# Last chunk of a long convolution: the place of one eviction on ScalarE, and a sum handed from VectorE to an accumulating transfer

## The chip, the cores and the metric

The kernel runs on one core of a Trainium2 chip. The metric is the device time of one execution in microseconds (us), given as the median of several runs. A core has five engines with an instruction queue each: TensorE (PE in the profile, its weight loads PEld), VectorE (DVE), ScalarE (ACT), GpSimd (POOL) and SyncE (SP). Matrix products land in PSUM and are copied out ("evicted") by ScalarE or VectorE. Transfers are issued by SP (queue q1 in the profile) or POOL (queue q0) and are carried out by sixteen DMA engines that all queues share.

## The reference

For 2048 positions and 1024 channels, two branches are mixed by a gate g = sigmoid(x · gate_w) of each position.

- Branch a is a diagonal state-space layer: `Bu = x @ B_bar.T`, the recurrence `h[t] = Lam_bar * h[t-1] + Bu[t]` (complex, 1024 states), then `a = 2 * Re(h @ C.T) + x * Dskip`.
- Branch b is a convolution over the whole sequence: k is convolved with four taps for each channel and multiplied by v, the product kv is convolved with `ssm_k` along the positions by a Fourier transform of twice the length, `kv * ssm_D` is added, and the result is multiplied by x.
- The output is `g * a + (1 - g) * b`, 1 x 2048 x 1024 in bf16.

## The kernel before

**Branch b** goes over the channels in eight chunks of 128. For a chunk, matmuls against tables of sines and cosines give the spectra K of the filter and V of kv, in four blocks. `products` (line 676) forms the spectrum G of their product on VectorE. It is a generator: each `yield` is a place where the caller may put other work. It multiplies first component by V into G, then the first component of the shifted blocks into W1 (one half of the work tile `wkh`), and adds W1 to blocks 1 to 3 of G. In all other chunks that sum is an accumulating transfer (`gather`, line 126, issued by POOL: 128 partitions x 2 x 1536 elements, 768 KB). In the last chunk, with `by_dma=False`, it is a tensor_tensor of 128x3072 on VectorE, four multiplications later. Blocks 2 and 3 of G then get one more sum, and four more operations of 128x2048 end the chunk's G. `inverse` (line 728) turns G back: eight matmuls into a PSUM tile `psz`, an eviction `cv` on ScalarE, a store of `cv` to a DRAM scratch by SP, and the same once more for the odd tiles.

**Branch a** is done in units of a block of 512 positions and a group of 256 states. `Bu(i)` makes two PSUM tiles named `both` (16 matmuls each, weights from `BT[g]`, which hold B for group g: first the eight matmuls with the real part, then eight with the imaginary part). ScalarE evicts each in two halves into `U`. `turn_U` (line 884) then scales U into `Q` on ScalarE in two steps, each followed by a `gather` of Q into U; the second transfer waits until the first has landed. VectorE runs the scans, and `Cy` multiplies by C: PSUM tile `psy`. `turn_C(pi)` (line 1266) mixes real and imaginary part of C's tile pi: two ScalarE operations into `m`, two more in place, and two gathers. C's first three tiles are called `CTa` in the trace.

**Order.** `put` (line 92) keeps each engine's instructions in the order of the program. PSUM is a pool of four tiles used in turn (line 81), so a PSUM tile is free again when the tile four places earlier has been evicted. The change lies in the block after the loop over the first seven chunks, which interleaves the last chunk's products (`prod`), the inverse of chunk 6 (`back`), the scaling of C's first two tiles (`turning[0]`, `turning[1]`), the gates of two position blocks (`gate`, 64 small matmuls in two PSUM tiles `p`, four tiny ScalarE operations) and the units Bu(6), Bu(7) and Bu(8). Before it, SP has been given the transposing loads of `CTa` 0 and 1, `BT[2]`, `BT[3]`, `CTa` 2 and `CT3`, in the order: CTa 0, BT[2], CTa 1, BT[3] (real, imaginary), CTa 2, CT3; then the two stores of `cv`, then the x of the last position block (`load_xT(3)`). Bu(7) is the first unit that uses BT[3].

Of the kernel before, what the change touches and what calls it, by code (L numbers as in the profile page):

```python
# [9 lines left out]
ALU = mybir.AluOpType  # L10
# [10 lines left out]
def kernel(  # L21
# [64 lines left out]
    def ps2(shape, name):  # L86
        return psum.tile(shape, F32, name=name, tag="ps")
# [4 lines left out]
    def put(eng, f, *a, **kw):  # L92
        with tc.issue_after(prev[eng]) if eng in prev else nullcontext():
            i = f(*a, **kw)  # L94
        prev[eng] = getattr(i, "ins", i)

    def mm(o, l, r, first, last):
        put("pe", nc.tensor.matmul, o, lhsT=l, rhs=r, start=first, stop=last)

    def bc(ap, shape):  # L100
        return ap.to_broadcast(shape)
# [3 lines left out]
    def tt(o, a, b, op):  # L105
        put("dve", V.tensor_tensor, out=o, in0=a, in1=b, op=op)
# [10 lines left out]
    def act(o, i, **kw):  # L117
        put("act", nc.scalar.activation, out=o, in_=i, **kw)
# [4 lines left out]
    def move(o, i):  # L123
        put("sp", nc.sync.dma_start, out=o, in_=i)

    def gather(o, i):
        put("pool", nc.gpsimd.dma_start, out=o, in_=i, accum_op=ALU.add)
# [122 lines left out]
    def load_xT(tb, halves=(0, 1), held=False):  # L250
        if tb not in xTs:
            xTs[tb] = (xt_pool if tb in (1, 2) else xt_first).tile([128, ND, TB], BF16, name="xT", tag="xT")
        for h in halves:
            if held:
                hold(xTs[tb][:, 0, h * HB:h * HB + 1])
            load_t(xTs[tb][:, :, h * HB:(h + 1) * HB], xf[tb * TB + h:(tb + 1) * TB:2, :])
# [201 lines left out]
    def turn_table(g):  # L458

        hr = u4([128, 2, 2, HB], F32, "hr")  # L460
        h, y = hr[:, 0], hr[:, 1]
        n = y.bitcast(I32)
        for o, rate in ((h, thn), (n, nthn)):
            for j in range(2):
                act(o[:, j], trow[0][:, 0:HB], func=ACT.Identity, scale=rate[:, 2 * g + j:2 * g + j + 1])
        yield
        gather(h, n)
        yield
        act(y, h, func=ACT.Abs)
        act(TS[:, 2 * g:2 * g + 2], h, func=ACT.Sin, scale=TWO_PI)  # L470
        act(TC[:, 2 * g:2 * g + 2], y, func=ACT.Sin, bias=pih, scale=-TWO_PI)
# [137 lines left out]
    def spectrum(which, c):  # L609
        if which == "K" and c % 2 == 0:  # L610

            t = BT[2].rearrange("p c d q -> p (c d q)")
        elif which == "G":
            t = whole[c] = g_pool.tile([128, 4096], BF16, name="G")
        else:
            t = kv_pool.tile([128, 4096], BF16, name=which + "h", tag="kvh")
        k = 2 if c == 0 else 1
        return [t[:, h * 4096 // k:(h + 1) * 4096 // k].rearrange("p (c b f d) -> p c b f d", c=2, b=4, d=128)
                for h in range(k)]
# [53 lines left out]
                    mm(ps[:, cc], tab[:, mt, fsl], eo[cc][:, mt], mt == 0, mt == 1)  # L673
            act(of_tile(VH[c], fi), ps, func=ACT.Copy, scale=2.0 / 1024.0)

    def products(c, h=0, home=u4, by_dma=True):

        if c not in GH:
            GH[c] = spectrum("G", c)
        K, Vt, G = (x[c][h].rearrange("p c b f d -> p c b (f d)") for x in (KH, VH, GH))  # L680
        w = K.shape[3]
        T2s = kv_pool.tile([128, 4096], BF16, name="t2", tag="kvh") if c == NC - 1 else BT[3].rearrange("p c d q -> p (c d q)")
        T2 = T2s[:, h * 2048:h * 2048 + 8 * w]
        W1, W2 = (WK[:, i, h * 1536:h * 1536 + 6 * w] for i in range(2))

        def mult(a, k, room, t=None):

            full = [128, 2, 4 - a, w]
            if t is None:
                t = room.rearrange("p (c b x) -> p c b x", c=2, x=w)  # L690
            tt(t, bc(K[:, k:k + 1, a:a + 1], full), Vt[:, :, 0:4 - a], ALU.mult)
            return t

        mult(0, 0, None, G)
        yield
        n1 = mult(1, 0, W1)
        if by_dma:
            gather(G[:, :, 1:], n1)
        yield
        t2 = mult(0, 1, T2)  # L700
        yield
        n2 = mult(1, 1, W2)
        if not by_dma:
            tt(G[:, :, 1:], G[:, :, 1:], n1, ALU.add)
        if c == NC - 1:
            yield
        n3 = mult(2, 1, home([128, 4 * w], BF16, "t"))
        tt(t2[:, :, 1:], t2[:, :, 1:], n2, ALU.add)
        n2 = mult(3, 1, home([128, 2 * w], BF16, "t"))
        tt(t2[:, :, 2:], t2[:, :, 2:], n3, ALU.add)  # L710
        n1 = mult(2, 0, W2[:, 0:4 * w])
        n3 = mult(3, 0, W2[:, 4 * w:])
        tt(t2[:, :, 3:], t2[:, :, 3:], n2, ALU.add)
        tt(n1[:, :, 1:], n1[:, :, 1:], n3, ALU.add)
        yield
        tt(G[:, :, 2:], G[:, :, 2:], n1, ALU.add)
        yield
        tt(t2[:, 1], G[:, 0], t2[:, 1], ALU.subtract)
        tt(t2[:, 0], G[:, 1], t2[:, 0], ALU.add)
        if c == 0 and h == 0:  # L720
            return
        lo, hi = ((t2[:, :, :, 0:256], t2[:, :, :, 256:512]) if c > 0 else
                  [T2s[:, i * 2048:(i + 1) * 2048].rearrange("p (c b x) -> p c b x", c=2, x=256) for i in range(2)])
        to = whole[c].rearrange("p (a c b x) -> p a c b x", a=2, c=2, b=4)
        tt(to[:, 0], lo, hi, ALU.subtract)
        tt(to[:, 1], lo, hi, ALU.add)

    def inverse(c):

        del GH[c]  # L730
        G = whole.pop(c).rearrange("p (a c b f d) -> p a c b f d", a=2, c=2, b=4, d=128)
        for par in range(2):
            ps = ps2([128, 2, 4, 128], "psz")
            for j in range(2):
                tl = 2 * par + j
                for fi in range(2):
                    for cc, tab in enumerate((CI, SI)):
                        mm(ps[:, j], tab[:, fi, tl * 128:(tl + 1) * 128], G[:, par, 1 - cc, :, fi],
                           fi == 0 and cc == 0, fi == 1 and cc == 1)
            cv = cv_pool.tile([128, 2, 4, 128], BF16, name="cv")  # L740
            act(cv, ps, func=ACT.Copy)
            move(cv_scr[c, :, 2 * par:2 * par + 2], cv)
            yield
# [16 lines left out]
    def gate(tb):  # L760
        psg = ps2([128, 2, 512], "p")[:, 0, 0:4]
        for tl in range(4):
            for dt_ in range(ND):
                mm(psg[:, tl:tl + 1], xTs[tb][:, dt_, tl * 128:(tl + 1) * 128], gwb[:, dt_:dt_ + 1],
                   dt_ == 0, dt_ == ND - 1)
        gates_of(slice(tb * 4, tb * 4 + 4), psg)
# [81 lines left out]
    turns_U = {}  # L848
# [208 lines left out]
    def step(gen):  # L1057
        next(gen, None)

    def run(gen):  # L1060
        for _ in gen:
            pass

    def steps(gen, n):
        for _ in range(n):
            step(gen)
# [35 lines left out]
    step(turns)  # L1102
    taps(1, dg1)
    p0 = products(0, 0)
    steps(p0, 3)
    tv = times_v(1)
# [17 lines left out]
    for c in range(NC - 1):  # L1124
        n, nn = c + 1, c + 2
        if c == 0:
# [3 lines left out]
            load_BT(0, 0)  # L1130
            load_xT(0, (0,))
            p1 = products(0, 1)
            fwd_K(n, (0, 1))
            step(p0)
# [25 lines left out]
        if c == 6:  # L1160
            put("pool", nc.gpsimd.tensor_copy, stamp, xTs[2][:, 0, 0:HB + 1:HB])
        tabs, back, prod = turn_table(c - 1) if c <= NG else none, inverse(c - 1), products(c)
        step(old)
        step(tabs)
# [91 lines left out]
    c = NC - 1  # L1256
# [36 lines left out]
    with tc.tile_pool(name="fin", bufs=1, side="right") as fin:  # L1293

        count = iter(range(16))

        def room(shape, dt, name):
            return fin.tile(shape, dt, name=name, tag=f"fin{next(count)}")

        prod, back = products(c, 0, room, False), inverse(c - 1)  # L1300
        run(old)
        steps(prod, 3)
        run(turns_U[3])
        run(next(tiles))
        steps(turning[0], 2)
        step(back)
        steps(turning[1], 2)
        run(back)
        gate(1)
        gate(2)  # L1310
        steps(prod, 2)
        b6, b7 = Bu(6)
        run(b6)
        run(b7)
        run(turns_U[6])
        run(turning[0])
        run(turning[1])
        run(prod)
        b8, b9 = Bu(7)
        run(b8)  # L1320
        run(b9)
        load_xT(3)
        b10, b11 = Bu(8)
        run(b10)
        run(b11)
    back = inverse(c)
# [208 lines left out]
```

## Time and profile before

| What | Value |
|---|---|
| time, median of 3 runs | 381.42 us (381.31 to 384.8) |
| the profiled execution's own time | 382.42 us |
| its span, first to last instruction | 380.6 us |
| PE busy | 370.4 us, 97% of the span |
| DVE busy | 369.1 us, 97% |
| ACT busy | 309.2 us, 81% |
| POOL busy | 81.8 us, 21% |
| granted TensorE clock | 0.999 |
| queue q1 (issued by SP) | 45.64 MB |
| queue q0 (issued by POOL) | 25.17 MB |

The span runs from the first to the last instruction of the core; the execution's time has 1.82 us around it. Busy shares are means over the span: two engines at 97% do not say which of them sets the end. A timeline row gives start, duration, engine, line (nearly all L94, the helper that records every operation), operation, `output<-inputs`, shapes and count, and in brackets the idle time before it with what ended it. Rows of one kind that follow each other are merged, so a merged row's duration covers all of them. Rows of the SP and POOL queues give the issue of a transfer, not its landing.

### The profile page before, as it was taken

To read this page: it belongs to the slowest core of one execution; us is meant where nothing else is said; L and a number is where in the kernel's file an instruction comes from. 1 tells how busy PE (TensorE), PEld (TensorE's weight loads), DVE (VectorE), ACT (ScalarE), POOL (GpSimd) and SP (SyncE) were. 2 spreads that over 40 slices of the span, in tenths; PEclk is the share of its full clock that TensorE was granted. 3 is DMA by queue.
4 is the path that set the end of the run, shared out by engine and by line. 5 is a ranking of instruction groups with operands and counts; after the bars stand their busy time and mean duration, and the time that the engine had idled before them with its cause. 6 is when DMAs were issued, how large, how long until landed. Compare 5 with 4: busy or idle time off the path is not lost.

```text
span 380.6 us, 6635 instructions
## 1 busy us (share of the span) xinstructions
PE 370.4 (97%) x2419; PEld 198.2 (52%) x2453; DVE 369.1 (97%) x593; ACT 309.2 (81%) x475; POOL 81.8 (21%) x111
## 2 busy tenths in 40 slices
PE   7999999999999999999989999999999999999996
PEld 4656357575574846644444444444444444444442
DVE  8899999999999999999999999999999999999995
ACT  5889996988979999786969699997988968948611
POOL 4011030110301103031002212223425322535000
PEclk9999999999999999999999999999999999999999
DMA  7979999999999998959998999976999999998902
GB/s 167 167 112 246 221 215 173 245 208 217 199 168 214 219 198 167 195 140 153 171 215 180 209 207 240 245 153 126 183 236 164 246 249 206 171 246 141 219 1 110
DMA packets 126403, 71.78 MB, mean 189 GB/s; under 512 B 104665, under 2 KB 107489, under 8 KB 126370
## 3 DMA queue, kind: packets, MB, share of 16 engines
q1 hardware_dynamic: 111232, 45.64, 56.2%
q0 software_dynamic: 12976, 25.17, 38.8%
q10 hardware_dynamic: 2162, 0.54, 0.8%
q8 instruction: 19, 0.31, 0.3%
q14 instruction: 14, 0.11, 0.1%
HBM read 15.48 MB, written 8.39 MB: 63 GB/s over the span
## 4 chain that ended last, share of the span: by engine, by line
PE 69%; DVE 15%; DMA 6%; issue 4%; ACT 3%; SPq 2%; ACTq 1%
PE psy L94 29%; PE both L94 17%; PE psk L94 6%; DVE BT L94 5%; DVE wkh L94 5%; PE psv L94 4%; PE taps L94 3%; PE foldk L94 3%; PE psz L94 3%; PE even L94 2%; DMA kT<-kT 2%; PE odd L94 2%; DVE G L94 2%; SPq L94 2%; ACT Vh L94 2%
## 5 line engine op out<-in xcount | busy, mean ns | idle before, releaser
L94 PEld LDWEIGHTS <-BT 128*128 128x128 bf16 x640 | 62.0, 98 | 49.5 <-issue 1.4
L94 PE MATMUL both<-xT,BT 128*128 128x512 bf16 x375 | 83.2, 379 | 1.4 <-ACT cv L94 1.0
L94 POOL DMA_DIRECT2D U<-Q x26 | 26.7, 1040 | 86.3 <-ACT Q L94 42.2
L94 PEld LDWEIGHTS <-hb 128*128 128x128 bf16 x256 | 25.0, 98 | 30.2 <-issue 0.5
L94 PEld LDWEIGHTS <-U 128*128 128x128 bf16 x240 | 23.5, 98 | 28.3
L94 PE MATMUL psy<-CT,hb 128*128 128x512 bf16 x157 | 36.5, 379 | 0.1
L94 ACT ACTIVATE Vh<-psv 128x1024 bf16<-128x1024 f32 x32 | 30.7, 1034 | 6.0 <-PE psv L94 6.0
L94 PE MATMUL psy<-CT,U 128*128 128x512 bf16 x148 | 34.6, 379 | 0.2
L94 DVE TENSOR_TENSOR_SCAN W<-rv,init,A 128x256 bf16<-128x256 f32 x48 | 32.1, 729 | 0.0
L94 POOL DMA_DIRECT2D G<-wkh x8 | 9.7, 1218 | 100.0 <-DVE wkh L94 100.0
L94 ACT ACTIVATE U<-both 128x512 bf16<-128x512 f32 x44 | 24.2, 594 | 8.3 <-PE both L94 8.0
L94 ACT ACTIVATE Q<-U,lam 128x512 bf16<-128x512 bf16 (+1 forms) x52 | 29.9, 612 | 0.0
L94 PE MATMUL psk<-eok,SF 128*128 128x384 bf16 (+1 forms) x119 | 28.2, 354 | 0.3
L94 PEld LDWEIGHTS <-SF 128*128 128x128 bf16 x184 | 18.0, 98 | 19.2 <-issue 0.5
L94 PE MATMUL psz<-G,CI 128*128 128x512 bf16 x64 | 24.3, 379 | 0.1
L94 PE MATMUL psz<-G,SI 128*128 128x512 bf16 x64 | 24.3, 379 | 0.0
L94 PE MATMUL psy<-CTa,hb 128*128 128x512 bf16 x94 | 22.6, 379 | 0.2
L94 PE MATMUL taps<-dg,kT 128*128 128x128 bf16 (+1 forms) x352 | 21.3, 207 | 1.4 <-DMA kT<-in_B_k_dram 1.0
L94 PEld LDWEIGHTS <-kT 128*128 128x128 bf16 x352 | 20.6, 98 | 3.2 <-DMA kT<-in_B_k_dram 2.0
L94 DVE TENSOR_TENSOR wkh<-BT,Vh 128x3072 bf16<-128x3072 bf16 (+4 forms) x20 | 21.8, 1109 | 0.0
L94 DVE TENSOR_TENSOR wkh<-Kh,Vh 128x3072 bf16<-128x3072 bf16 (+2 forms) x16 | 21.2, 1347 | 0.0
L94 PE MATMUL psy<-CTa,U 128*128 128x512 bf16 x87 | 20.6, 379 | 0.1
(230 smaller groups left out, 846.8 us busy)
## 6 DMA issues: line engine op xcount, KB each, us to landing
U<-Q POOLq DMA_DIRECT2D x26, 256.0 KB, 5.2
G<-wkh POOLq DMA_DIRECT2D x6, 768.0 KB, 8.8
cv_scr<-cv SPq DMA_DIRECT2D x16, 256.0 KB, 7.7
kn<-in_B_ssm_k_dram SPq DMA_DIRECT2D x5, 512.0 KB, 3.8
v<-in_B_v_dram SPq DMA_DIRECT2D x5, 512.0 KB, 6.4
out_dram<-m SPq DMA_DIRECT2D x8, 256.0 KB, 4.6
BT<-cv_scr SPq DMA_DIRECT2D x7, 256.0 KB, 6.3
out_dram<-BT SPq DMA_DIRECT2D x7, 256.0 KB, 2.0
```

Source lines behind the costliest of these rows:

```text
L94: i = f(*a, **kw)
```

## The change

In the last chunk the sum of W1 into blocks 1 to 3 of G becomes a `gather`, issued right after W1's multiplication, as in the other chunks; the tensor_tensor goes, and with it the parameter `by_dma`. `run(turns_U[3])` (eight ScalarE operations into Q, two gathers) comes ahead of the first three steps of `prod` in the program, so that on POOL its two gathers stand ahead of the new one; VectorE's and ScalarE's own orders are not touched by that. `run(back)`, which holds the second half of the inverse of chunk 6 (eight matmuls, the eviction `cv` on ScalarE, SP's store), comes ahead of `steps(turning[1], 2)`, the first two ScalarE operations on C's tile 1. PE's and SP's orders stay as they are.

```diff
-    def products(c, h=0, home=u4, by_dma=True):
+    def products(c, h=0, home=u4):
...
         n1 = mult(1, 0, W1)
-        if by_dma:
-            gather(G[:, :, 1:], n1)
+        gather(G[:, :, 1:], n1)
         yield
         t2 = mult(0, 1, T2)
         yield
         n2 = mult(1, 1, W2)
-        if not by_dma:
-            tt(G[:, :, 1:], G[:, :, 1:], n1, ALU.add)
         if c == NC - 1:
             yield
...
-        prod, back = products(c, 0, room, False), inverse(c - 1)
+        prod, back = products(c, 0, room), inverse(c - 1)
         run(old)
+        run(turns_U[3])
         steps(prod, 3)
-        run(turns_U[3])
         run(next(tiles))
         steps(turning[0], 2)
         step(back)
+        run(back)
         steps(turning[1], 2)
-        run(back)
         gate(1)
         gate(2)
         steps(prod, 2)
```

## The prediction

> **What bounds the kernel now.** The page's chain of work that ended last is 69% PE, and read in order of time it is PE without a break from 196.3 us to 377.1 us; then one VectorE operation and the last store. So up to 377 us a microsecond counts only if PE gets it. I read the table of waits next, for 180 to 225 us, where the change lies (line waited for, total, times, longest). PE has one:
>
> ```profile
> PE both L94 <- ACT cv L94: 1.0, 1, 1.0
> ```
>
> Then the timelines of that place, PE, its weight loads, ACT:
>
> ```profile
> 191.75 3.61 PE L94 MATMUL both<-xT,BT 128*128 128x512 bf16 x15
> ...
> 196.32 17.43 PE L94 MATMUL both<-xT,BT 128*128 128x512 bf16 x79 [0.96 <-ACT cv L94]
> ...
> 194.98 0.10 PEld L94 LDWEIGHTS <-BT 128*128 128x128 bf16 x1
> 196.32 9.59 PEld L94 LDWEIGHTS <-BT 128*128 128x128 bf16 x45 [1.24 <-issue]
> ...
> 188.50 2.18 ACT L94 ACTIVATE m<-CTa,mc2i 128x1024 bf16<-128x1024 bf16 x2
> 190.57 1.01 ACT L94 ACTIVATE cv<-psz 128x1024 bf16<-128x1024 f32 x1
> 193.17 2.19 ACT L94 ACTIVATE m<-CTa,mc2i 128x1024 bf16<-128x1024 bf16 x2 [1.59 <-DMA CTa<-in_A_C_im_dram]
> 195.27 1.00 ACT L94 ACTIVATE cv<-psz 128x1024 bf16<-128x1024 f32 x1
> ```
>
> The second `cv` frees the PSUM tile of Bu(6)'s second `both`. Its matmuls had ended at 190.3, but ACT stood first at C's tile 1, whose load landed at 193.15, and evicted at 195.27 to 196.27; PE waited. Weight loads of one unit follow each other every 0.216 us (0.098 busy, 0.118 idle), so of the 1.24 us idle 1.12 are lost.
>
> Two more places matter later, ACT's timeline, then PE's:
>
> ```profile
> 213.20 0.22 ACT L94 ACTIVATE U<-ends 128x4 bf16<-128x4 bf16 x1 [2.44 <-DMA U<-Q]
> ...
> 217.24 1.02 ACT L94 ACTIVATE cv<-psz 128x1024 bf16<-128x1024 f32 x1 [0.57 <-PE psz L94]
> ...
> 250.50 2.06 ACT L94 ACTIVATE U<-both 128x512 bf16<-128x512 f32 x4
> ...
> 251.64 0.81 PE L94 MATMUL psy<-CTa,hb 128*128 128x512 bf16 x3
> ```
>
> From 217.24 to 252.5 ACT shows no idle time. The second of those four evictions ends at about 250.50 + 0.49 + 0.58 = 251.57 and frees the PSUM tile of the first `psy`, which starts at 251.64, 0.07 us later than PE's rhythm asks. ACT and PE are tied there: PE keeps a gain only if ACT's row from 217.24 on moves up too.
>
> **The change, part by part.**
>
> *The second cv ahead of C's tile 1.* ACT idles 1.59 us before 193.17; cv (0.92 from start to start) fits in at 191.5 and ends at 192.5. C's tile 1 still starts at 193.17, since its load decides, and the gates follow 0.92 us sooner. The next `both` starts at 194.98 + 0.22 = 195.20: **-1.12 us** on PE. What is late next: Bu(7)'s first tile needs the gate's PSUM tile, freed at about 195.5, and starts at 195.20 + 16 x 0.216 = 198.65. No wait there.
>
> *The sum off VectorE.* The row that goes:
>
> ```profile
> 195.42 1.75 DVE L94 TENSOR_TENSOR G<-G,wkh 128x3072 bf16<-128x3072 bf16 x1
> 197.09 1.21 DVE L94 TENSOR_TENSOR t<-Kh,Vh 128x2048 bf16<-128x2048 bf16 x1
> ...
> 204.68 1.23 DVE L94 TENSOR_TENSOR G<-G,wkh 128x2048 bf16<-128x2048 bf16 x1
> ```
>
> VectorE gains 197.09 - 195.42 = 1.67 us, none of it at the end by itself: PE uses G at 213.58, 2.9 us after its last write (210.69), and no later PE row waits for VectorE. I cost it at nothing. Cover: those 2.9 us, and near the end the last `hb`, done at 367.0, which PE needs four matmuls into its row of 367.41, at about 368.3.
>
> *The new transfer.* W1 is written at 191.63. POOL issues turns_U[3]'s transfers at 186.10 and 190.95 (0.86 us), so the gather issues at 191.8. That is what the move of turns_U[3] is worth: behind the gather, the transfer of 186.10 would have waited 5.7 us. Nothing else is queued on POOL until 202.87. The page has its like in other chunks:
>
> ```profile
> G<-wkh POOLq DMA_DIRECT2D x6, 768.0 KB, 8.8
> ```
>
> The six land 6.5 to 10.0 us after issue: 198.3 to 201.8 here. The sum that waits for it moves to 204.68 - 1.67 = 203.0, so the new wait is covered by 1.2 to 4.7 us; past that, VectorE's later products and scans are queued behind it, and PE would notice from 3.6 us of lateness on (212.5 against 209.0).
>
> *What the transfer pushes aside.* The DMA view in quarters of a microsecond shows how q0 and q1 take turns. From 194.75 to 195.5 the second U<-Q moves 0.04 to 0.06 MB a quarter and q1 nothing at all, although BT[3]'s imaginary half was at issue from 192.47; that half then runs at 0.07 a quarter from 195.75 to 197.6. A gather of this size, at 123 to 126 us, runs at 0.05 a quarter and q1 is at zero: 3.9 us. So transposing loads and gathers alternate as wholes. Who goes first at 195.75? The nearest row is 212.5 us: one U<-Q ended, four CTa<-m gathers had been issued from 208.37 on, and q1's x transpose ran first (212.5 to 214.3). By that row BT[3] keeps its place, and the gather runs 197.6 to 201.5 and lands near 202.1, still before 203.0. I take this.
>
> *What comes after.* The loads of CTa 2 and CT3 and the stores of `cv` move back by up to 3.9 us; C's tile 2 is not touched by ACT before 220.98, and the scratch is read from 225.97 on. But turns_U[6]'s two transfers share these queues, and ACT waits for the second at 213.20. Its first goes out about 1.0 us sooner (202.87 to 201.9). DMA was idle for 1.5 us (206.5 to 208.0) and 0.5 us (200.5 to 201.0), so of the 3.9 us some 2.0 are absorbed; the second transfer can slip in ahead of the x transpose (landing near 211) or wait behind it (up to 214.2). After landing, ACT needs 217.24 - 0.57 - 213.20 = 3.47 us to the last `cv`, and PE's psz allows it from 217.24 - 1.12 = 216.12. Landing by 212.65: all 1.12 us kept. Landing as now, 213.20: 216.67 against 217.24, so 0.57 kept. From 213.77 on: nothing, and at 214.2 ACT is 0.4 late.
>
> **The sum.** I take the middle of full gain and landing as now: (1.12 + 0.57) / 2 = 0.85, say **-0.8 us**. Against the profiled execution: span 380.6 to 379.8, time 382.42 to 381.6. Its median is 1.0 us lower than that execution, so **380.6 us**.
>
> **The rivals.**
>
> *A. The gather goes ahead of BT[3] (slower).* Place: Bu(7)'s imaginary matmuls. If q0 keeps its turn at 195.75, as the four CTa<-m gathers do among themselves (214.25 to 219.5, with cv's store issued at 216.69 held until 219.5), the gather ends at 199.65, BT[3]'s second half runs 1.85 us to 201.5 and lands 0.6 to 1.5 later (0.6 between last data and landing of the U<-Q of 190.95; 1.45 for CTa 1): 202.1 to 203.0. PE needs it at 198.65 + 8 x 0.216 = 200.4. It decides from 200.4 + 1.12 = 201.5 on: later than that, PE loses more than it won. Net -1.12 + 1.7 to 2.6 = +0.6 to +1.5: **382.0 to 382.9 us**. For it: q1 stood at zero while a gather ran. Against: the row at 212.5.
>
> The Trainium skill (DMA: Bandwidth & Descriptors, section Queues, rings and completion order) says that each DMA engine goes round between the queues that have work, a packet at a time. By that rule both streams would share from 195.75 on, BT[3]'s half would take 2 x 1.85 us to 199.5, and rival A could not occur; the sum would stay. The trace bears the turns out but not their size: 0.00 MB of q1 beside 0.05 of q0 in a quarter at 195.0.
>
> *B. The late turn, or nothing.* turns_U[6]'s second transfer lands at 213.8 or later, ACT's unbroken row keeps its place and the tie at 251.6 gives the gain back, or the freed PSUM tile isn't what PE lacks at 195.2. **381.4 us**, up to 381.8. For it: a tie of 0.07 us and 3.9 us more DMA time ahead of it. Against: ACT idles 2.44 us there now, and the transfers start sooner.
>
> *C. More than that.* All 1.12 us pass, and VectorE's 1.67 us help at a later tie that the waits don't show: **379.8 to 380.3 us**.
>
> **How the numbers follow.** Forecast (379.9 to 381.0, with C) 0.5; B 0.25; A 0.2; anything else 0.05: a second collision of the kind of A, such as xT or CT loads late for their first use. The range for 8 in 10 takes in C's end and A's: **379.7 to 382.9**. A measurement of this kernel tells about 1%, 3.8 us, from no change. No case above reaches that; three runs of the same kernel spread by 3.5 us and the unknown collision is left: faster 0.04, same 0.88, slower 0.08.
>
> **What would show it.** After: no PE wait for `cv` near 195, the next `both` at 195.2; `cv` twice in a row on ACT from 190.57; a G<-wkh issue on POOL at 191.8, landing by 203; no G<-G,wkh of 128x3072; VectorE's sum at 203.0 without a wait. A shows as PE waiting for a BT load at 198 to 202; B as ACT's U<-ends at 213.8 or later and the first `psy` still at 251.6. Wrong altogether: a PE gap where before shows none.

## The result, and the profile after

| | before | after |
|---|---|---|
| median of 22 runs each, side by side | 382.22 us (381.26 to 391.18) | 385.92 us (382.4 to 394.96) |
| profiled execution: time, span | 382.42 us, 380.6 us | 384.49 us, 382.7 us |

The ratio after/before is **1.0055, interval 1.0031 to 1.0078**: some 2.1 us slower, 1.2 to 3.0. The ratio leaves out executions more than 1.5% above the fastest of their kernel, 2 of the 22 before and 7 of the 22 after, which the medians in the table include. Put on the 381.42 us of the prediction, the ratio gives 383.5 us. The prediction was 380.6 us, its range ended at 382.9: the sign was wrong, and the time lay outside the range. It lies within the 1% that one comparison of this kernel tells from no change, and the interval, which comes from many runs, excludes 1.

The table of waits of the kernel after, from 176 us on (line waited for, total, times, longest), for PE and its weight loads:

```profile
PE both L94 <- DMA BT<-in_A_B_im_dram: 1.9, 1, 1.9
PEld L94 <- DMA BT<-in_A_B_im_dram: 2.4, 1, 2.4
```

The wait for `cv` is gone, as the change meant, and a longer one for BT[3]'s imaginary half stands in its place. The timelines of PE, ACT, POOL and SP show both:

```profile
191.76 1.92 ACT L94 ACTIVATE cv<-psz 128x1024 bf16<-128x1024 f32 x2
193.57 2.19 ACT L94 ACTIVATE m<-CTa,mc2i 128x1024 bf16<-128x1024 bf16 x2
...
192.82 8.79 PE L94 MATMUL both<-xT,BT 128*128 128x512 bf16 x40
203.54 12.26 PE L94 MATMUL both<-xT,BT 128*128 128x512 bf16 x56 [1.93 <-DMA BT<-in_A_B_im_dram]
...
191.89 0.86 POOL L94 DMA_DIRECT2D U<-Q  x1 [3.75 <-ACT m L94]
192.72 1.26 POOL L94 DMA_DIRECT2D G<-wkh  x1
...
192.28 5.27 SPq L94 DMA_TRANSPOSE BT<-in_A_B_im_dram  x1
```

`cv` comes twice in a row, and PE runs 40 matmuls from 192.82 without a gap. At the 41st, the first with BT[3]'s imaginary part, it stops for 2.1 us against its rhythm of 0.216. SP needed 5.27 us to issue that load, against 3.81 before. The chain of work that ended last goes through the load:

```profile
192.28 11.22 DMA BT<-in_A_B_im_dram
203.50 0.05 issue
203.54 12.26 PE both L94 x56
```

The load took 11.2 us from issue to landing. The DMA view of three stretches, 195.2 to 198.25, 198.25 to 201.2 and 201.2 to 201.69 us (queue: packets, MB, share of the engines' time), shows why:

```profile
q1 hardware_dynamic: 2048, 0.52, 89.3%
q0 software_dynamic: 81, 0.16, 35.1%
...
q0 software_dynamic: 192, 0.59, 102.9%
...
q0 software_dynamic: 30, 0.09, 96.6%
...
q1 hardware_dynamic: 15, 0.00, 4.2%
```

BT[3]'s half does get its turn ahead of the gather, as forecast, and all of its data goes through: the half is 256 x 1024 numbers in bf16, 0.52 MB, and that is what q1 moved up to 198.25. Then the gather had the engines, and q1 moved nothing for 3 us. What was missing until then is the end of the load: in the trace, the data of each transposing load of this stretch is followed by 32 packets of 4 bytes, and those of BT[3]'s half ran from 201.22 to 202.77, behind the gather. PE went on at 203.54. (Which packet belongs to which load is read from order and number. Eight other loads of this execution whose landing the trace has landed 0.4 to 1.7 us after their last such packet.)

By the rule from the Trainium skill that the prediction weighed (DMA: Bandwidth & Descriptors, section Queues, rings and completion order), the engines would have gone on serving q1 packet by packet beside q0; in this execution q1 stood still from 198.25 to 201.2. Other executions agree with the rule, counted in the trace's packets: in `sum_only`, below, 160 packets of q1 ran beside 160 of q0 from 195.75 to 198.25 us, and in `after_2` 96 beside 93 from 199 to 200.5. A load is held up even so, for its packets are of 256 bytes and the gather's of some 3 KB: 0.04 MB beside 0.49 in `sum_only`. Why q1 stood still in the one and not in the others stays open.

That is one execution. Further executions of both kernels, shown below, tell that the wait for BT is one of three places where the gather comes out, and that the wait for `cv` is not in every execution of the kernel before.

To compare executions I use **the stretch**: from the start of the gates' matmuls (`p`) to where the chain leaves PE for the last VectorE operation, both read from the trace. Before: 190.14 to 377.11, 186.97 us. After: 191.13 to 379.17, 188.04 us. The 1.0 us by which the gates start later lies ahead of the change, where both kernels have the same order.

### The profile page after: what moved, and what is told of

It reads as the page before. It is cut to its first block, busy times and chain, and to the rows that moved or that the text cites. A ratio compares the mean times of both kernels' runs of the same rounds, so it can differ in the third digit from the quotient of the medians.

```text
span 382.7 us, 6671 instructions
## 1 busy us (share of the span) xinstructions
PE 373.0 (97%) x2453; PEld 199.2 (52%) x2453; DVE 367.8 (96%) x592; ACT 309.6 (81%) x475; POOL 82.2 (21%) x112
## 4 chain that ended last, share of the span: by engine, by line
PE 66%; DVE 17%; DMA 9%; issue 4%; ACT 3%; ACTq 1%; SPq 0%; DVEq 0%
PE psy L94 29%; PE both L94 16%; DVE BT L94 6%; PE psk L94 6%; DVE wkh L94 5%; PE taps L94 3%; PE psv L94 3%; DMA BT<-in_A_B_im_dram 3%; DVE G L94 2%; PE foldk L94 2%; PE even L94 2%; DMA kT<-kT 2%; DMA kT<-in_B_k_dram 2%; PE odd L94 2%; PE psz L94 2%
## 5 line engine op out<-in xcount | busy, mean ns | idle before, releaser
L94 PEld LDWEIGHTS <-BT 128*128 128x128 bf16 x640 | 61.9, 98 | 50.7 <-DMA BT<-in_A_B_im_dram 2.4
L94 PE MATMUL both<-xT,BT 128*128 128x512 bf16 x384 | 83.9, 379 | 1.9 <-DMA BT<-in_A_B_im_dram 1.9
L94 POOL DMA_DIRECT2D U<-Q x26 | 26.2, 1018 | 85.0 <-ACT Q L94 31.8
L94 PEld LDWEIGHTS <-hb 128*128 128x128 bf16 x256 | 24.9, 98 | 30.2 <-issue 0.5
L94 PEld LDWEIGHTS <-U 128*128 128x128 bf16 x240 | 23.5, 98 | 28.3
L94 PE MATMUL psy<-CT,hb 128*128 128x512 bf16 x160 | 36.8, 379 | 0.0
L94 ACT ACTIVATE Vh<-psv 128x1024 bf16<-128x1024 f32 x32 | 30.7, 1034 | 5.6 <-PE psv L94 5.6
L94 PE MATMUL psy<-CT,U 128*128 128x512 bf16 x152 | 34.9, 379 | 0.0
L94 ACT ACTIVATE U<-both 128x512 bf16<-128x512 f32 x44 | 24.3, 594 | 11.5 <-PE both L94 11.3
L94 POOL DMA_DIRECT2D G<-wkh x9 | 11.0, 1223 | 100.0 <-DVE wkh L94 100.0
L94 DVE TENSOR_TENSOR_SCAN W<-rv,init,A 128x256 bf16<-128x256 f32 x48 | 32.2, 731 | 0.0
L94 ACT ACTIVATE Q<-U,lam 128x512 bf16<-128x512 bf16 (+1 forms) x52 | 29.9, 613 | 0.0
L94 PE MATMUL psk<-eok,SF 128*128 128x384 bf16 (+1 forms) x120 | 28.5, 354 | 0.0
L94 PEld LDWEIGHTS <-SF 128*128 128x128 bf16 x184 | 18.0, 98 | 18.8
L94 PE MATMUL taps<-dg,kT 128*128 128x128 bf16 (+1 forms) x352 | 22.2, 212 | 2.1 <-DMA kT<-kT 2.0
L94 PE MATMUL psz<-G,CI 128*128 128x512 bf16 x64 | 24.3, 379 | 0.0
L94 PE MATMUL psz<-G,SI 128*128 128x512 bf16 x64 | 24.3, 379 | 0.0
L94 PEld LDWEIGHTS <-kT 128*128 128x128 bf16 x352 | 21.4, 101 | 3.9 <-DMA kT<-kT 1.3
L94 PE MATMUL psy<-CTa,hb 128*128 128x512 bf16 x96 | 22.7, 379 | 0.0
L94 DVE TENSOR_TENSOR wkh<-BT,Vh 128x3072 bf16<-128x3072 bf16 (+4 forms) x20 | 21.8, 1110 | 0.0
L94 DVE TENSOR_TENSOR wkh<-Kh,Vh 128x3072 bf16<-128x3072 bf16 (+2 forms) x16 | 21.3, 1351 | 0.0
L94 PE MATMUL psy<-CTa,U 128*128 128x512 bf16 x88 | 20.6, 379 | 0.0
```

## The experiments

**One part alone.** The first pair splits the change. `sum_only` keeps the gather and the place of turns_U[3], and puts the second eviction back behind C's tile 1:

```diff
-        run(back)
         steps(turning[1], 2)
+        run(back)
```

> The changed kernel with the second eviction cv back behind C's tile 1, so the accumulating transfer alone. Theory 1, BT[3]: the last part of BT[3]'s imaginary half waits behind the new transfer, so it lands about 11 us after its issue and Bu(7) waits for it. PE also keeps its old 1.12 us wait for cv, but that one is now followed by the wait for BT[3], which ends at the same time as in the changed kernel: the time is the changed kernel's, +1.3 to +2.1 us against before, and PE waits about 0.8 to 1.0 us for BT[3] instead of 1.93. Rival, order of ScalarE: the loss comes from the eviction's new place, so without it the time is that of before or lower, 0 to -1 us.

Measured: 1.0044 (1.001 to 1.0078), stretch 188.55 us. PE's timeline:

```profile
195.51 5.34 PE L94 MATMUL both<-xT,BT 128*128 128x512 bf16 x24 [0.16 <-ACT cv L94]
203.04 12.26 PE L94 MATMUL both<-xT,BT 128*128 128x512 bf16 x56 [2.19 <-DMA BT<-in_A_B_im_dram]
```

The transfer alone brings the wait for BT and nearly the whole loss. The wait is longer than expected, 2.19 us for 0.8 to 1.0. Here the gather was already at work when the load's data began, at 195.30, which is rival A's order. The DMA view from 195.75 to 198.25:

```profile
q0 software_dynamic: 160, 0.49, 100.8%
q1 hardware_dynamic: 160, 0.04, 12.4%
```

The load's last data ran at 200.83, after the gather. And the wait for `cv`, with the eviction in its old place, is 0.16 us here and not 0.96: a first sign that it varies.

`cv_only` is the kernel before with that one swap, the sum staying on VectorE:

```diff
-        steps(turning[1], 2)
         run(back)
+        steps(turning[1], 2)
```

> Before with only the second eviction cv moved ahead of C's tile 1; the sum stays on VectorE, no new transfer. Theory 1: no wait for BT[3], no wait for cv, PE gains 1.12 us near 195; the tie with ScalarE at 251.6 lets 0.6 to 1.1 us of it through: -0.6 to -1.1 us. Rival, order of ScalarE: slower than before, +1 us or more.

> The kernel with only the second cv moved, once more, for the interval: -0.6 to -1.1 us against before (ratio 0.997 to 0.9985), 185.9 us from the gates' first matmul to PE's last one.

Measured: 0.9979 (0.9951 to 1.0007), and in the repeat 1.0007 (0.9972 to 1.0042). PE runs all 96 matmuls of the three units through in both, stretches 185.95 and 185.94 us. Repeat, PE's timeline:

```profile
192.76 20.88 PE L94 MATMUL both<-xT,BT 128*128 128x512 bf16 x96
```

So the swap does take the wait away, 1.02 us against the first execution of the kernel before, and still no gain is measured: the two intervals, -1.9 to +0.3 us and -1.1 to +1.6 us, hold nothing at all as well as the gain that was expected. More executions of the kernel before, below, tell more.

**The gather later.** `w1_last` has the whole change, but in the last chunk W1's multiplication, and so the gather, comes after the one into W2 (POOL issues it at 196.43 instead of 192.72):

```diff
-        n1 = mult(1, 0, W1)
-        gather(G[:, :, 1:], n1)
+        if c < NC - 1:
+            n1 = mult(1, 0, W1)
+            gather(G[:, :, 1:], n1)
...
         n2 = mult(1, 1, W2)
+        if c == NC - 1:
+            n1 = mult(1, 0, W1)
+            gather(G[:, :, 1:], n1)
```

> The changed kernel with VectorE's four multiplications of the last chunk in another order, W1's last, so that the accumulating transfer is issued about 3.9 us later (195.6 instead of 191.8). Same work, same transfers. Theory 1: BT[3]'s second half is through before the transfer starts (198), Bu(7) does not wait; the transfer lands near 203.5, VectorE waits 0.5 to 1.5 us for it, which PE does not see: -0.6 to -1.1 us against before. Rival, the transfer's mere volume (loads of the whole stage are late, wherever it is issued): +1 to +2 us like the changed kernel.

Measured: 1.0008 (0.9965 to 1.005), stretch 186.28 us. No wait for BT; VectorE waited 1.0 us for the gather. A small wait of PE has come up at the other end, at the first `psy` (`PE psy L94 <- ACT U L94`, 0.3 us), after turns_U[6]'s second transfer had landed at 213.59.

**The gather smaller.** `third` gathers block 1 alone (256 KB) and leaves blocks 2 and 3 to VectorE, 128x2048:

```diff
-        gather(G[:, :, 1:], n1)
+        gather(*((G[:, :, 1:], n1) if c < NC - 1 else (G[:, :, 1], n1[:, :, 0])))
...
         if c == NC - 1:
+            tt(G[:, :, 2:], G[:, :, 2:], n1[:, :, 1:], ALU.add)
             yield
```

> The changed kernel with only block 1 of the sum (256 KB instead of 768 KB) by accumulating transfer, blocks 2 and 3 added by one VectorE operation of 128x2048 (1.22 us). Theory 1: the transfer takes 1.3 instead of 3.9 us, so BT[3]'s second half lands 2.6 us sooner, at about 200.9 on the clock of the profile before, and PE waits 0 to 0.5 us for it: -1.1 to -0.3 us against before. Rival, order of ScalarE: as the changed kernel, +1.3 to +2.1.

Measured: 0.9995 (0.9963 to 1.0027), stretch 187.67 us in the profiled execution. No wait for BT. That the gather's size is the reason is not shown by it: BT[3]'s half was issued early here, from 190.31 on in 2.02 us, its data was through by 195.4, and `after_2` and `after_3`, below, have no such wait with the whole 768 KB. ACT's and PE's timelines show the second place:

```profile
214.51 0.22 ACT L94 ACTIVATE U<-ends 128x4 bf16<-128x4 bf16 x1 [4.95 <-DMA U<-Q]
...
252.26 2.75 PE L94 MATMUL psy<-CTa,hb 128*128 128x512 bf16 x12 [1.67 <-ACT U L94]
```

`split3` issues the 768 KB as three gathers of 256 KB:

```diff
+        for b in range(3 if c == NC - 1 else 0):
+            gather(G[:, :, 1 + b], n1[:, :, b])
+        if c < NC - 1:
             gather(G[:, :, 1:], n1)
```

> The changed kernel with the 768 KB transfer issued as three of 256 KB, one for each block. If the two queues take turns transfer by transfer: BT[3]'s tail runs after the first piece, 2.6 us sooner, PE waits 0 to 0.3 us for it, and VectorE may wait up to 2 us for the last piece, unseen: 186.0 to 186.6 us from the gates' first matmul to PE's last one, unless the late turn costs up to 1.7. If queue 0 keeps its turn as long as it has transfers: PE waits 1.9 to 2.4 us for BT[3] as in the changed kernel, 188 us.

Measured: 396.14 us for the profiled execution, 384.23 for the fastest of six and 391.98 to 395.1 for the other four, so there is no ratio and nothing follows for the time. Its order can be read: BT's row on SP took 1.98 us, PE did not wait for BT but 7.1 us for ACT, and VectorE waited 5.9 us for the sum's transfers.

**The loads in another order.** `bu8_first` takes Bu(8), which uses BT[2], ahead of Bu(7), and loads the last x behind both, so that BT[3] is needed a unit later (32 matmuls of 0.216 us, 6.9 us):

```diff
-        b8, b9 = Bu(7)
+        b8, b9 = Bu(8)
         run(b8)
         run(b9)
-        load_xT(3)
-        b10, b11 = Bu(8)
+        b10, b11 = Bu(7)
         run(b10)
         run(b11)
+        load_xT(3)
```

> The changed kernel with the units Bu(7) and Bu(8) exchanged (and the load of the last x behind both), so that BT[3] is needed 6.9 us later; the transfer of 768 KB stays. Theory 1, BT[3]'s tail: nobody waits for BT[3] any more although it lands as late as in the changed kernel (about 203.5); from the gates' first matmul to PE's last one it takes 186.0 to 186.5 us (before 186.97, changed kernel 188.04): -0.5 to -1.0 us. Rival, the transfer hurts elsewhere too: 187.5 us or more.

Measured: 1.0114 (1.008 to 1.0147), stretch 190.49 us. No wait for BT, and yet the highest ratio of the study. (BT[3]'s half ended as in the kernel after: its last data ran at 197.35, its 4-byte packets at 199.65 to 200.15, behind the gather.) ACT's timeline, then PE's:

```profile
210.82 0.22 ACT L94 ACTIVATE U<-lam 128x4 bf16<-128x4 f32 x1 [1.01 <-DMA U<-Q]
...
228.54 2.19 ACT L94 ACTIVATE Q<-CT,mc2i 128x1024 bf16<-128x1024 bf16 x2 [2.27 <-DMA CT<-in_A_C_im_dram]
...
253.84 4.24 PE L94 MATMUL psy<-CTa,hb 128*128 128x512 bf16 x12 [2.82 <-ACT U L94]
```

This is a third place. On SP the loads of C's later tiles stand behind x; x went out later (212.81), C's next tile with it, and ACT waited 2.27 us for it inside the row that the prediction called unbroken. PE pays at the first `psy`. The edit itself put x later, and no run has this order without the gather, so how much of the loss is the gather's is not shown.

`third_held` is `third` with x loaded behind both units, held back:

```diff
-        load_xT(3)
         b10, b11 = Bu(8)
         run(b10)
         run(b11)
+        load_xT(3, held=True)
```

> The 256 KB kernel (third) with the load of the last x held back until Bu(8)'s evictions, so that turns_U[6]'s second transfer does not queue behind it. Theory, late turn: ScalarE's U<-ends then waits under 2.5 us instead of 4.95, the first psy no longer waits for ScalarE (1.67 us in third), and from the gates' first matmul to PE's last one it takes 185.9 to 186.4 us (third: 187.67). Rival, ScalarE's stretch from 217 to 252 is late for another reason: the 1.7 us wait stays.

Measured: 1.006 (1.0024 to 1.0095), stretch 192.03 us. ACT waited 1.77 us for C's tile (and 2.06 for the store of `cv`), PE 0.98 and then 2.82 us for ACT; a wait of 0.54 us for BT came besides. Taking x out of the gather's way only moves the loss to C.

**More executions of both kernels, nothing changed.** These were to tell which of the places belongs to the change and which to one execution.

> The changed kernel once more. Theory (the tail of BT[3]'s imaginary load, cut off by the 768 KB gather, sets PE's stall): PE waits for a BT imaginary load near 202 us again, with 1.5 to 3.5 us depending on how much of the load is still to be issued when the gather takes its turn, and the stretch from the gates' first matmul to PE's last matmul is 187.6 to 189.6 us against 186.97 in the kernel before. Rival (the one profiled execution was an accident, and the extra time comes from ahead of the change's place): no such wait or one under 1 us, a stretch of 186 to 187 us, and the gates starting later than 190.5 us by as much as the time is longer. Ratio of times by the theory 1.002 to 1.006; by the rival as before, 1.0055, with a short stretch.

> The kernel before once more, one look. Theory: the stretch from the gates' first matmul to PE's last matmul repeats at 186.9 to 187.1 us, since PE has no other wait in it than the one of about 1.0 us for cv; the start of the gates, which hangs on load landings earlier in the execution, may move by 1 to 2 us. Rival (the stretch itself varies from execution to execution by a microsecond or more): a stretch off by over 0.5 us, with a wait that the first look did not show.

> A third look at the changed kernel. Theory: a PE wait for BT's imaginary load of 1.5 to 3.5 us near 202 us, the stretch from the gates to PE's last matmul 187.6 to 189.6 us, and longer by just as much as the wait is longer. Rival (accident): no wait of over 1 us there.

> A third look at the kernel before. Theory: stretch of 186.9 to 187.1 us again; the start of the gates anywhere between 189.9 and 192.4 us, as it was in the runs so far. Rival: the start of the gates stays within 0.2 us of 190.14 in all three looks, so that a later start in the kernels with the early eviction belongs to that edit.

> The kernel before, a fourth look. New theory: in most executions PE has no wait at all between the gates and its last matmul (stretch 185.9 to 186.1 us); the 1.0 us for cv, which the prediction set out to save, appears only where CTa 1's load lands later than 191.9 us, as in the first profile (193.15), and the stretch is then 186.97. So no wait and 186.0 us here, or a wait and a late CTa 1 together. Rival (the wait belongs to the order of the kernel, whatever the load does): a wait of 1.0 us although CTa 1 landed before 192 us.

> The changed kernel, a fourth look. New theory: the gather costs PE in one of two places, never in both fully. Either BT[3]'s imaginary load takes over 4 us to be issued, and PE waits 1.5 to 2.5 us for it near 202 us (stretch 187.5 to 188.6); or it is issued in some 2 us, ahead of the gather, and then the second transfer of turns_U[6] lands later than 213.8, ScalarE's unbroken row starts late, and the first psy waits 0.5 to 1.2 us (stretch 186.5 to 187.2). Rival (neither is the gather's doing): a stretch of 186.0 us with both waits absent.

> The kernel before, a fifth look. New theory: as in the fourth look: a stretch of 185.9 to 186.1 us without a wait if CTa 1 has landed by 192 us, or 186.9 to 187.1 with the wait for cv if not; U<-ends at 210.5 to 213.2 and no wait of PE for ScalarE's U. Rival: a wait of 1.0 us although CTa 1 landed before 192 us, or a psy that waits without any gather in the stretch.

> The changed kernel, a fifth look. New theory: as in the fourth look: one of the two places, BT near 202 us with a stretch of 187.5 to 188.6 us, or the first psy near 252 us with 186.5 to 187.2; which one follows from whether the row of BT[3]'s imaginary load on SP takes over 4 us or about 2. Rival: a stretch of 186.0 us with neither.

| execution | time, us | gates start | stretch | PE's wait in it |
|---|---|---|---|---|
| before | 382.42 | 190.14 | 186.97 | `cv`, 1.0 |
| before_2 | 381.50 | 190.14 | 186.04 | none |
| before_3 | 381.60 | 190.35 | 185.94 | none |
| before_4 | 381.42 | 190.13 | 185.95 | none |
| before_5 | 382.39 | 190.16 | 186.91 | `cv`, 0.9 |
| after | 384.49 | 191.13 | 188.04 | BT, 1.9 |
| after_2 | 383.01 | 190.52 | 187.18 | first `psy`, 1.2 |
| after_3 | 382.73 | 190.87 | 186.54 | first `psy`, 0.6 |
| after_4 | 385.21 | 191.10 | 188.79 | first `psy`, 2.8 |

(after_5 took 395.52 us and is left out of the table and of the means below. PE waits there for ACT, 7.1 us at `both` and 2.8 at the first `psy`, and not for BT.)

Before: in three of the five executions PE does not wait at all, against the expectation of the first two repeats. ACT's timeline in before_4, then PE's:

```profile
190.76 1.01 ACT L94 ACTIVATE cv<-psz 128x1024 bf16<-128x1024 f32 x1
191.66 2.18 ACT L94 ACTIVATE m<-CTa,mc2i 128x1024 bf16<-128x1024 bf16 x2
193.74 1.01 ACT L94 ACTIVATE cv<-psz 128x1024 bf16<-128x1024 f32 x1
...
191.82 20.88 PE L94 MATMUL both<-xT,BT 128*128 128x512 bf16 x94
```

C's tile 1 had landed in time, so the second `cv` ended by 194.75 although it came second. In before_5 the tile was late, and the wait is back:

```profile
193.12 2.19 ACT L94 ACTIVATE m<-CTa,mc2i 128x1024 bf16<-128x1024 bf16 x2 [1.50 <-DMA CTa<-in_A_C_im_dram]
...
196.26 17.43 PE L94 MATMUL both<-xT,BT 128*128 128x512 bf16 x79 [0.88 <-ACT cv L94]
```

The early eviction is therefore worth 1.0 us in some executions and nothing in the others; a stretch without any wait is 185.9 to 186.0 us, which `cv_only` reached twice, and the kernel before three times without the swap.

After: the wait for BT, expected of the first two repeats, came in none, and the expectation of two places was too few. In after_2 and after_3 BT's imaginary half was issued in 2.0 us (SP's rows of 191.10 and 191.35), and PE did not wait for it. Instead turns_U[6]'s second transfer was late. ACT and PE in after_3:

```profile
214.20 0.22 ACT L94 ACTIVATE U<-ends 128x4 bf16<-128x4 bf16 x1 [3.78 <-DMA U<-Q]
...
251.94 2.75 PE L94 MATMUL psy<-CTa,hb 128*128 128x512 bf16 x12 [0.56 <-ACT U L94]
```

In after_4 it was C's next tile, as in `bu8_first`, here with the order of the change itself. ACT, PE, and two rows of SP that stand ahead of the tile; in before_4 they took 1.16 and 9.46 us:

```profile
229.12 2.19 ACT L94 ACTIVATE Q<-CT,mc2i 128x1024 bf16<-128x1024 bf16 x2 [2.73 <-DMA CT<-in_A_C_im_dram]
...
254.42 2.75 PE L94 MATMUL psy<-CTa,hb 128*128 128x512 bf16 x12 [2.76 <-ACT U L94]
...
200.66 4.70 SPq L94 DMA_TRANSPOSE CT<-in_A_C_re_dram  x1
208.27 11.58 SPq L94 DMA_TRANSPOSE xT<-in_A_x_dram  x2
```

Counted from the gates, the loads of C's next tile began to be issued at 30.1 us there, at 27.7 to 28.7 in the five executions of before and at 28.0 in both of `cv_only`. The length of the x row does not tell them apart, it was 11.02 us in `cv_only` too; its start does in part, 17.2 us after the gates in after_4, 15.7 in `cv_only` and 15.7 to 16.7 in the kernel before. In the first execution of the kernel after and in `sum_only` C's loads were as late, at 30.6 and 30.5, but ACT, 2.1 and 2.6 us late behind PE's wait for BT, found the tile there: one wait covers the other.

What room there was to catch up shows in the table by stage, 190 to 222 us (span, then busy time and count of PE, its weight loads, VectorE, ScalarE, POOL; then granted clock, DMA share, GB/s). First before_4:

```profile
190.00:222.00 32.00, 31.84 (x203) 15.36 (x205) 31.69 (x42) 26.28 (x47) 6.96 (x8) 1.00 1.04 200
```

Then after_4:

```profile
190.00:222.00 32.00, 31.84 (x203) 15.44 (x205) 31.54 (x43) 26.07 (x48) 8.20 (x9) 1.00 1.17 212
```

A share of 1 and more means that the packets, taken together, took as long as the sixteen engines had. In the kernel before there is a pause: the share falls to 0.55 from 202 to 207 us in before_4, to 0.68 in before_3 and 0.89 in before_2, and from 207 to 212 to 0.85 in the first execution and 0.88 in before_5. After, no such stage lies below 0.96. I take this for the room in which late loads were made good and which the gather fills; no run tests it.

**The second place has a law.** Take the start of `U<-ends`, which waits for turns_U[6]'s second transfer, against the start of the gates, in executions in which PE has no other wait:

| execution | `U<-ends` after the gates, us | wait of the first `psy`, us |
|---|---|---|
| before_2 | 22.80 | 0 |
| w1_last | 23.06 | 0.33 |
| after_3 | 23.33 | 0.56 |
| after_2 | 23.95 | 1.15 |
| third | 24.45 | 1.67 |

From 22.8 us on, each microsecond that the transfer lands later costs PE one, within 0.1 us. It arrives through ACT's row, which has no idle time up to the first `psy`.

**Adding up.** The means of the table of executions: stretch 186.36 us before (five) and 187.64 after (four), +1.28; gates 190.18 and 190.91, +0.72; together +2.0, beside +2.1 by the ratio. The four stretches after lie 0.6 to 2.8 us above the 185.95 of a stretch without waits, 1.7 in the mean: that is the gather's price in these four. The swap gives back 0.41 (186.36 - 185.95). The later start of the gates is not explained: all executions of before lie within 190.13 to 190.35, those after within 190.52 to 191.13, but `third` and `sum_only`, which have a gather, started at 190.06 and 190.13, and `cv_only`, without one, at 192.39. No row ahead of the gates differs in order, and PE's waits there, mostly for loads, lie in the first 60 us, at 93 us (0.37 us, in some) and at 152 to 156 us (one of 0.4 to 1.0 us in each execution of either kernel), so chance in so few executions is possible. It stays open, and with it a third of the sum.

The four do not stand for all: of the fifteen executions behind the ratio, five took 385.6 to 387.0 us at a granted clock of 0.994 to 0.996, and the four ran at 0.999 and more. `bu8_first` and `third_held`, profiled at 0.994, show what such an execution can hold, in the last section.

One execution does not always stand for its kernel: `third` (stretch +1.3 against the mean before, ratio -0.2 us, interval -1.4 to +1.0) and `third_held` (+5.7, ratio +2.3, interval +0.9 to +3.6) had a profiled execution worse than their mean.

No version is shown to be faster than the kernel before: `cv_only`, `third` and `w1_last` cannot be told from it.

## Why the prediction was wrong, step by step

- **The wait for cv (-1.12 us).** Right as a mechanism, wrong as a gain of the kernel. The profiled execution had the wait; three of the five executions do not. The prediction's own numbers held the warning: it noted that the median was 1.0 us below that execution, and then took the gain off the median as well. That median, of three executions, is the time of one without the wait: those took 381.42 to 381.60 us, those with it 382.39 and 382.42. It was also low: the medians of 22, 35 and 27 later executions were 382.22, 382.63 and 382.57. Averaged over the five executions the gain is 0.4 us, a third of the term. **This is one of the two steps that failed.**
- **The sum off VectorE at nothing.** Held. With the sum on VectorE, `cv_only` reaches the stretch without waits. (The lateness that PE would notice, 3.6 us in the prediction, is 3.5 by its own 212.5 and 209.0.)
- **The gather's issue and landing.** Issue 192.72 against 191.8; the gates, too, started 1.0 us later. Landing 11.0 us after issue, at 203.7, beyond the 6.5 to 10.0 of the six others; VectorE waited 0.25 us for it, and PE took no harm.
- **"BT[3] keeps its place, and the gather runs 197.6 to 201.5".** The order and the gather's duration were right: BT[3]'s data was through by 198.2, and the gather ran from 198 to 201.5. **The other step that failed is that the place was enough**, that the load would land soon after its data. The prediction allowed 0.6 to 1.45 us from the last data to the landing; it was 5.3 us, from 198.2 to 203.5, since the load's last packets of 4 bytes went behind the gather. The price is rival A's (+0.6 to +1.5 forecast, +1.07 in the stretch of the first profile), by another route than rival A's, which let the gather go first. In `sum_only` it did go first. There the two queues were served packet by packet, which by the prediction could not bring rival A, because it took equal turns for equal shares of the time (2 x 1.85 us); at 0.04 MB beside 0.49 the load's data took 5.5 us, and PE waited 2.19.
- **What comes after, and rival B.** The tie at 251.6 and its bounds were right. The prediction had the gain begin to go for landings after 212.65, which is 22.5 us after the gates; measured 22.8. But B was taken to end at +0.4, because it was set against a PE that had a wait to lose. Against a PE without one, the same lateness costs 0.6 to 1.2 us (after_3 and after_2).
- **The loads of CTa 2 and CT3 "moved back by up to 3.9 us" at no cost.** True of those two, whose uses are late. What stands behind them on SP, x and then C's next tile, was only named as a possible collision in the last 0.05 of the chances. It cost 2.8 us in after_4 and comes up again in `bu8_first`. "Of the 3.9 us some 2.0 are absorbed" came from pauses that other executions have too, but the rest was not followed to the end of SP's queue.
- **The range.** Its upper end, 382.9, was rival A's price on the median. The places were priced one by one, each net of a gain that the median did not have. Without it, A alone gives 1.7 to 2.6 us, 383.1 to 384.0, and the result's 383.5 lies in the middle. That it does so is in part luck: only one of the four executions lost at A's place, and 0.7 us of the loss is the unexplained start of the gates.

## What to carry to other kernels

Before a wait in a profile is taken off a time, ask whether the time has it: where the profiled execution lies above the median by about as much as the wait is worth, profile a second execution first. A transfer added to a stretch in which the DMA engines are nearly full is not paid at its own landing, but at whichever load behind it has the least slack, so the queue has to be followed to its last use, in this case 36 us further on. And a load whose data is through ahead of another transfer has not thereby landed ahead of it: look for the landing itself, or for the engine that waits for it.

## What the runs showed of the hardware

- A transposing load can be held up by a gather in two ways. Its data can be through and its end not: in the kernel after 2048 packets of 256 bytes ran up to 198.2 us, 32 of 4 bytes from 201.22 to 202.77, behind the gather, and PE waited until 203.5. Or the two share packet by packet, and the one with small packets moves little: 160 packets and 0.04 MB beside 160 and 0.49 MB in 2.5 us of `sum_only`. Over the four executions of the table the load's row on SP took 1.96 to 5.27 us, and the wait goes with it: 1.9 us of wait at 5.27, none at 1.96, 2.03 and 3.21.
- A pause of 2.82 us on PE brought the granted clock down to half. The table by stage of `bu8_first` (PE, weight loads, VectorE, ScalarE, POOL, then clock, DMA share, GB/s) shows it:

```profile
245.00:250.00 5.00, 5.00 (x25) 2.25 (x24) 3.97 (x8) 4.97 (x7) 0.00 (x0) 1.00 1.14 256
250.00:254.00 4.00, 1.18 (x6) 0.49 (x5) 3.97 (x10) 3.97 (x8) 1.71 (x2) 0.93 0.97 227
254.00:256.00 2.00, 2.00 (x6) 0.67 (x5) 1.97 (x6) 2.00 (x6) 0.00 (x0) 0.50 1.00 169
256.00:258.00 2.00, 2.00 (x9) 0.84 (x8) 1.97 (x8) 2.00 (x4) 0.00 (x0) 0.78 0.03 8
```

The twelve matmuls after it took 4.24 us instead of 2.75, so the pause cost 1.5 us more than its length; in `third_held` it was 4.17 us after 2.82. After 2.76 us in after_4 the clock stayed at 1.00 and the twelve took 2.75. The Trainium skill (TensorE: Matmul & The Clock Gate, section Part 1: The HAM clock gate) lets the clock fall after an idle window of about 3.4 us; these rows show it after a shorter pause.
